# Duo attention and a two-layer MLP in one program: chunk order, V buffers, load order, and seven products in one more chunk

## The chip, the cores and the metric

The kernel runs on one core of a Trainium2 chip. A core has TensorE (PE) for matrix products, VectorE (DVE), ScalarE (ACT), GpSimd (POOL) and SyncE (SP), which work side by side and meet through semaphores. Transfers are issued by SP, ACT and POOL and are carried out by the core's 16 DMA engines. The metric is the device time of one execution in microseconds. Before the change its median is 223.92 us over three runs (223.15 to 224.44).

## The reference

Attention runs over 4 batches, 8 heads, 768 positions and 64 elements per head. Heads 0, 2 and 6 see all earlier positions; the other five see the first 4 positions (the sinks) and a window of 64. The attention's output, 3072 rows of 512, goes through two matrices with a leaky ReLU between them.

```python
scores = scale * np.matmul(q, k.transpose(0, 1, 3, 2))
causal = rel >= 0
stream_keep = causal & (is_sink | in_win)
mask = np.where(retr[0, :, 0, 0, None, None], full_mask, stream_mask)
a = np.exp(scores); a = a / (np.sum(a, axis=-1, keepdims=True) + 1e-09)
x = attn_out.transpose(0, 2, 1, 3).reshape(B * S, H * D)
h = x @ w_in                      # 512 -> 2048
g = np.maximum(0.01 * h, h)
return g @ w_out                  # 2048 -> 512
```

## The kernel before

**Chunks.** The rows are cut into 8 chunks of 384: two halves c = 0 and c = 1 of each batch. `ORDER` says which (batch, half) stands at which place. Before the change the order is, within each pair of batches, both first halves and then both second halves: (0,0) (1,0) (0,1) (1,1) (2,0) (3,0) (2,1) (3,1). A second half sees twice as many keys, so its attention is longer: a head that sees everything has five units (a unit is a product of queries and keys, an exponential, and later the product with V) where in a first half it has two. With the five window heads and one sink unit this makes 21 units in a second half and 12 in a first one.

**Stages of a chunk.** POOL loads Q, K and V and casts them (`load_qk`, `load_v`). SP turns K and Q with transposing transfers (`turn_dma`), VectorE spreads K into two zero-padded halves (`spreads`). SP copies V shifted by 64 rows into a second tile (`v_shift`, from `va` to `vb`), which the window heads need. Attention (`Attention.slots`) is a list of slots: slot t holds the score product and exponential of unit t, and the product with V of unit t - lag. When a pair of heads is done, VectorE divides by the row sums (`finish`, into `xs`), and SP turns the result into `xt` with a transposing transfer (`x_t`). Then comes the first matrix, `in_slots`: 16 ticks of four matmuls of 384 columns, each followed on ACT by the leaky ReLU into `g_all`. The second matrix runs in `Pair`s of two row tiles by a seven-product scheme (14 steps of four matmuls of 256 columns for a pair), with sums of `g_all` on VectorE, and its result goes out from the `o` tiles by SP.

**Seven products for the first matrix.** For the chunks in `BY_SEVEN` (6 and 7), half of the ticks, those of the first two groups of four column tiles, are replaced by a `Quad` each: seven units of four matmuls of 192 columns, with sums of w_in (`in_sums`, four on VectorE in pass 4, kept in the tiles of V buffer 1) and sums of xt (`x_sums`), copies on ACT and additions on VectorE.

**The order of work is written out by hand.** Each engine runs its instructions strictly in program order. Chunks 0 and 1 are written line by line. Then pass n, for n = 2 to 7 of the main loop (before.py, `for n in range(2, NCH)`), holds chunk n's first matrix (`ins`), the attention of chunk n+1 (`a`), the second matrix of what chunk n-1 completed (`outs`: one pair after an even chunk, two after an odd one), and the preparation of chunk n+2 and the loads of chunk n+3. `merge` spreads the slots of `a` evenly over the time of `ms`; the last microseconds of `ms` are kept back (`keep`) so that attention ends before the pass does. At the end of passes 3 and 4 POOL holds until the last `xt` of chunk n+1 has landed, and then issues Q and V of chunk n+3.

**Queues.** SP runs, for each pass, in order: the turning of K and Q of chunk n+2, the two shifted copies of its V, the four `xt` transposes of chunk n+1, the stores. An issue that waits holds what stands behind it. The same holds for POOL's loads. V has three buffers (batch 3 uses batch 0's).

**Lines** in the profile: L597 ticks, L679 units of a Quad, L771 and L792 steps of the second matrix, L357 and L392 score products, L326 products with V, L362 and L397 exponentials, L401 window masks, L425 `xs`, L430 `xt`, L248 turned K and Q, L153 and L154 shifted copies, L126 loads of V, L119 loads of K and Q, L143 loads of w_in, L637 and L646 sums of w_in and xt, L706 additions of a Quad, L600 the leaky ReLU, L826 stores.

Of the kernel before, what the change touches and what calls it, by code (L numbers as in the profile page):

```python
# [17 lines left out]
CH = 384  # L18
# [3 lines left out]
def kernel(  # L22
# [33 lines left out]

    ORDER = [(b + e, c) for b in range(0, B, 2) for c in range(2) for e in range(2)]

# [3 lines left out]
    def bf(name, *shape):  # L62
        return one.tile([128, *shape], BF16, name=name)
# [5 lines left out]
    ident = bf("ident", 128)  # L69
    blank = bf("blank", 256)  # L70
    diff = bf("diff", 128)
    half = one.tile([128, 2], FP32, name="half")
    m_caus = bf("m_caus", 128)
    n_caus = bf("n_caus", 128)
    n_one = bf("n_one", 64)
    n_first = bf("n_first", 128)
    m_one = bf("m_one", 64)
# [3 lines left out]
    hold = bf("hold", 1)  # L81
    shift = bf("shift", 2, 128)
    kt = [[bf(f"kt{i}_{hh}", 4, S) for hh in range(2)] for i in range(2)]
    va = [bf(f"va{i}", 6, H, D + 1) for i in range(3)]
    vb = [bf(f"vb{i}", 5, H - 1, D + 1) for i in range(3)]
    va.append(va[0])
    vb.append(vb[0])
    vs = [bf(f"vs{i}", H, D + 1) for i in range(2)]
# [13 lines left out]
    q0 = rot.tile([128, 3, H, D], BF16, name="q0", tag="qd", bufs=3)  # L102
    f0 = {nm: rot.tile([128, DM], FP32, name="o", tag="o", bufs=5).rearrange("p (h d) -> p h d", h=H) for nm in ("k", "q")}

# [136 lines left out]

    def turn_dma(n):
        qx[n] = rot.tile([128, 3, 4, 128], BF16, name="qd", tag="qd", bufs=3)
        raw["kx", n] = rot.tile([128, 3, 4, 128], BF16, name="kd", tag="kd", bufs=2)
        for nm, dst in (("k", raw["kx", n]), ("q", qx[n])):
            thirds = [slice(j, j + 1) for j in range(1 if nm == "q" and n == 3 else 3)]
            for g in thirds if n < 4 or (nm, n) == ("k", 4) else [slice(0, 3)]:
                nc.sync.dma_start_transpose(out=dst[:, g].rearrange("p g q t -> p (g q) t"),  # L248
                                            in_=raw[nm, n][:, g].rearrange("p g h d -> p (g h d)"))
# [333 lines left out]
    done = [0] * NCH  # L583
    BY_SEVEN = (6, 7)

# [7 lines left out]
    def in_slots(n, tags=("ph",)):  # L593
        def tick(t, tag=None):
            ph = bank(tag or tags[t % len(tags)], [128, 512], FP32)
            for g in range(KG):
                nc.tensor.matmul(ph[:, 0:CH], lhsT=w_in_bf[:, g, 128 * t : 128 * t + 128],  # L597
                                 rhs=xts[n][:, g, :] if n else xts[0][:, :, g, :], start=(g == 0), stop=(g == KG - 1))
            done[n] += 1
            nc.scalar.activation(out=g_all[:, slab(n) : slab(n) + 3, t, :],  # L600
                                 in_=ph[:, 0:CH].rearrange("p (j t) -> p j t", j=3), func=ACTF.Prelu, alpha=0.01)

        if n not in BY_SEVEN:
            return [costing(0.65, lambda t=t: tick(t)) for t in range(NG)]
        ticks = [costing(0.65, lambda t=t: tick(t)) for t in range(NG // 2, NG)]
        if n + 1 < NCH:
            ticks = [costing(0.65, lambda t=t: tick(t)) for t in range(NG // 2, NG)]
            r, left = [], []
            for k in range(2):
                *units, last = Quad(n, k, "ph").slots()  # L610
                for x, f in enumerate(units):
                    r += [f, *left] if x == 1 else [f]
                    if x in (0, 1, 2, 5):
                        r.append(ticks.pop(0))
                left = [last]
            return r + left

        both = zip(Quad(n, 0, "psS").slots(), Quad(n, 1, "po").slots())
        return [f for t, two in zip(ticks, both) for f in (t, *two)]

    KH = KG // 2
    in_sum = {}
    for i, t in ((1, va[1]), (3, vb[1])):
        t = t.rearrange("p g h d -> p (g h d)")[:, 0 : 2 * KH * 512].rearrange("p (x g c) -> p x g c", x=2, g=KH)
        in_sum[i], in_sum[i + 1] = t[:, 0], t[:, 1]

    def in_sums(i):


        def quarter(a, e):  # L630
            w = w_in_bf[:, KH * a : KH * a + KH, 0:1024].rearrange("p g (k e f) -> p g k e f", e=2, f=256)
            return w[:, :, :, e, :]

        part = lambda j: in_sum[j].rearrange("p g (k f) -> p g k f", f=256)
        x, y, op = {1: (quarter(0, 1), quarter(1, 1), ALU.add), 2: (part(1), quarter(0, 0), ALU.subtract),
                    3: (quarter(0, 0), quarter(0, 1), ALU.subtract), 4: (quarter(1, 0), part(2), ALU.subtract)}[i]
        nc.vector.tensor_tensor(part(i), x, y, op=op)  # L637
# [3 lines left out]
    def x_sums(n):  # L641
        x = xts[n].rearrange("p g (j e t) -> p g j e t", j=3, e=2)
        b = lambda a, e: x[:, KH * a : KH * a + KH, :, e, :]
        t = rot.tile([128, 4, KH, 3, 64], BF16, name="x_sum", tag="qb", bufs=1)
        for i, y, z in ((1, b(0, 1), b(0, 0)), (2, b(1, 1), t[:, 0]), (3, b(1, 1), b(0, 1)), (4, b(1, 0), t[:, 1])):
            nc.vector.tensor_tensor(t[:, i - 1], y, z, op=ALU.subtract)  # L646
        x_sum[n] = t
        temps[n] = [rot.tile([128, 2, CH], FP32, name=nm, tag=tag, bufs=bufs) for nm, tag, bufs in
                    (("p1s", "kd", 2), ("us", "kd", 2), ("u3s", "kb", 1))]

    class Quad:
# [9 lines left out]
        def unit(self, u):  # L661
# [6 lines left out]
            w = lambda a, e: w_in_bf[:, KH * a : KH * a + KH, 512 * k + 256 * e : 512 * k + 256 * e + 256]  # L668
            q = lambda i: in_sum[i][:, :, 256 * k : 256 * k + 256]
            lhs, rhs, at = {"P1": (w(0, 0), b(0, 0), "y"), "P2": (w(1, 0), b(1, 0), "a"), "P6": (q(2), t[:, 1], "y"),  # L670
# [21 lines left out]
        def empty(self, u, s):  # L692
            copy = lambda o: nc.scalar.activation(out=o, in_=s, func=ACTF.Copy)
            if u == "P1":
                self.left = 4
                self.p1, self.u, self.u3 = (t[:, self.k] for t in temps[self.n])
                copy(self.p1)
# [39 lines left out]
    class Pair:  # L737
# [42 lines left out]
        def unit_of_two(self, u, half, lo, hi):  # L780
# [17 lines left out]
            if u == "P1":  # L798
                self.o = [rot.tile([128, DM], FP32, name="o", tag="o", bufs=5) for _ in range(2)]
                self.p1 = self.temp("p1", 2)  # L800
# [27 lines left out]
        def empty(self, u, s, c0, c1):  # L828
            add = lambda o, t: nc.vector.tensor_tensor(o, s, t[:, c0:c1], op=ALU.add)
            if u == "P1":  # L830
                self.o = [rot.tile([128, DM], FP32, name="o", tag="o", bufs=5) for _ in range(2)]
                self.p1 = self.temp("p1", 2)
# [116 lines left out]
    load_qk(1, "q")  # L949
    load_in(768, 1024)  # L950
    load_v(1)
    load_in(1024, 1536)
    load_in(1536, 2048)
# [100 lines left out]
    p0 = in_slots(0)  # L1054
    a1 = Attention(1, score_tags=("py", "psS", "psS"), po_tags=("po", "po", "po", "py"), xt_eng="v").slots([0, 2, 6, 1, 3, 4, 5, 7], lag=6)

# [7 lines left out]
    for a in ats[2:]:  # L1064
        nc.vector.memset(a[:, :, 1:3, :], 0.0)
    run(a1[5:7])
    v_shift_pe(0, "ph", "v", 1)
    run(a1[7:8])
    v_shift_pe(1, "ph", "v", 1)
    run(a1[8:11], merge(p0[8:], a1[11:]))  # L1070
    nc.vector.tensor_copy(m_win[:], m_one.rearrange("p (o t) -> p o t", o=1).to_broadcast([128, 6, 64]))
    zero_keys(0, nc.vector, CH, S)
    zero_keys(1, nc.vector, CH, S)
    nc.vector.memset(va[2][:, :, :, D], 1.0)
    turn_dma(2)
# [11 lines left out]
    load_qk(4)  # L1087
    load_v(4)
    run(steps(1, ("P1",)))
# [18 lines left out]
    sp, keep = spreads(3), tail(m2[at:], a2[-7:])  # L1108
    run(keep[:-5], sp[:3], keep[-5:], sp[3:])

    for n in range(2, NCH):
        a, extra = [], ()
        if n + 2 < NCH:
            if ORDER[n + 2][1] == 0:
                load_sinks(ORDER[n + 2][0])
                sink_values(ORDER[n + 2][0], nc.gpsimd)
            turn_dma(n + 2)
            v_shift(n + 2)
            extra = spreads(n + 2)
            if n + 3 < NCH:  # L1120
                load_qk(n + 3, "k" if n > 2 else "kq")
                if n < 3:
                    load_v(n + 3)
        if n + 1 < NCH:
            a = Attention(n + 1, cross=True).slots(lag=2 if n > 3 else 3)
            a = into(a, extra) if n > 2 else a
        if n == 4:
            more = [lambda i=i: in_sums(i) for i in range(1, 5)]
            a = [f for j, s in enumerate(a) for f in ([s, more[j // 2 - 1]] if j in (2, 4, 6, 8) else [s])]
        ins = in_slots(n)  # L1130
# [4 lines left out]
        elif n == 4:  # L1135
            ms = outs[:8] + ins[:2] + merge(ins[2:], outs[8:-6]) + outs[-6:]
        elif n == 6:
# [6 lines left out]
        if n == 2:  # L1144
            run(ms[:1])
            ms = ms[1:]
            at = last_of(ms, 3.5)
            ms, keep = ms[:at], tail(ms[at:-2], a[-3:]) + ms[-2:]
            a = a[:-7] + [f for i in range(4) for f in (a[i - 7], *extra[2 * i : 2 * i + 2])]
        elif a:  # L1150
            at = last_of(ms, 3.2 if n == 3 else 5.8)
            ms, keep = ms[:at], ms[at:]
            if n > 4:
                keep.insert(1, a.pop())
        run(merge(ms, a), keep)
        if n in (3, 4):

            nc.gpsimd.tensor_copy(hold[0:1, :], xts[n + 1][0:1, 3, 0:1])
            if n > 2:
                load_qk(n + 3, "q")  # L1160
            load_v(n + 3)
# [37 lines left out]
```

## Time and profile before

| what | value |
|---|---|
| median of three runs | 223.92 us (223.15 to 224.44) |
| profiled execution, its own time | 225.39 us |
| its span, first to last instruction | 223.6 us |
| granted TensorE clock | 1.000 |
| TensorE busy | 214.8 us, 96% |
| ACT busy | 144.6 us, 65% |
| VectorE busy | 139.7 us, 62% |
| POOL busy | 72.3 us, 32% |
| read from HBM, written | 27.30 MB, 6.29 MB |
| chain that ended last, by engine | PE 66%, DMA 22%, POOL 8% |

The page lists busy times, the span in 40 slices, the DMA queues and a chain: from the last instruction back, at each step to what released it. Groups and timelines name a line, an engine, the tiles written and read, a count and a time; what stands after `<-` in brackets ended the idle time before the instruction. All times are microseconds from the span's start.

### The profile page before, as it was taken

How to read it: one execution, taken by the hardware profiler on the slowest of the kernel's cores; microseconds unless marked ns; L12 is line 12 of the kernel's file. 1: busy time of each engine (PE TensorE's matmuls, PEld its weight loads, DVE VectorE, ACT ScalarE, POOL GpSimd, SP SyncE). 2: the span in 40 equal slices, each digit the busy share in tenths (PEclk: the TensorE clock that was granted, in tenths of full speed). 3: DMA queues.
4: the chain of work that ended last, by engine and by line, in shares of the span. 5: the costliest groups of instructions: out<-in, count | busy, mean ns of one | idle time of the engine just before them, and what ended most of it. 6: DMA issues, size and time to landing. Idle time of an engine off the chain costs nothing.

```text
span 223.6 us, 5996 instructions
## 1 busy us (share of the span) xinstructions
PE 214.8 (96%) x2408; PEld 167.6 (75%) x2408; DVE 139.7 (62%) x383; ACT 144.6 (65%) x329; POOL 72.3 (32%) x89
## 2 busy tenths in 40 slices
PE   8899999999899899989999999999999999999994
PEld 5578766688698576876687777677787988888893
DVE  6686967949599355851775773455383756707653
ACT  4767947743686897367647644888658886487220
POOL 8988632079208512821419300800000000000000
PEclk9999999999999999999999999999999999999999
DMA  9999999999999999999999995999320130200222
GB/s 129 159 179 169 196 206 179 180 152 154 130 115 198 212 108 149 130 201 159 146 186 145 127 148 148 159 139 145 73 94 4 55 95 18 97 0 3 94 94 97
DMA packets 112203, 28.89 MB, mean 129 GB/s; under 512 B 102192, under 2 KB 109232, under 8 KB 112176
## 3 DMA queue, kind: packets, MB, share of 16 engines
q0 software_dynamic: 77552, 13.37, 88.7%
q1 hardware_dynamic: 33568, 14.88, 37.5%
q8 instruction: 19, 0.31, 0.6%
q10 hardware_dynamic: 1056, 0.26, 0.6%
q14 instruction: 8, 0.07, 0.1%
HBM read 27.30 MB, written 6.29 MB: 150 GB/s over the span
## 4 chain that ended last, share of the span: by engine, by line
PE 66%; DMA 22%; POOL 8%; issue 1%; ACT 1%; DVE 0%; POOLq 0%; ACTq 0%
PE ph L597 26%; PE py L792 18%; DMA va<-in_v_dram 6%; PE po L326 6%; DMA w_in_bf<-in_moe_w_in_dram 4%; POOL va L126 4%; PE psS L357 4%; DMA kb<-in_k_dram 3%; DMA kd<-kb 3%; DMA xt<-xs 3%; DMA vb<-va 2%; PE ph L679 2%; PE py L771 2%; PE po L792 2%; PE psS L392 1%
## 5 line engine op out<-in xcount | busy, mean ns | idle before, releaser
L597 PE MATMUL ph<-xt,w_in_bf 128*128 128x384 bf16 x384 | 75.7, 326 | 0.8 <-DMA xt<-xs 0.7
L600 ACT ACTIVATE g_all<-ph 128x384 bf16<-128x384 f32 x96 | 47.1, 490 | 27.3 <-PE ph L597 26.0
L597 PEld LDWEIGHTS <-w_in_bf 128*128 128x128 bf16 x416 | 37.4, 97 | 18.6 <-issue 0.7
L362 ACT ACTIVATE at<-psS 128x384 bf16<-128x384 f32 x76 | 35.8, 489 | 8.9 <-PE psS L357 5.4
L792 PEld LDWEIGHTS <-sum 128*128 128x128 bf16 x256 | 23.9, 98 | 4.4
L119 POOL DMA_DIRECT2D kb<-in_k_dram x21 | 18.8, 918 | 22.4 <-DMA kd<-kb 21.3
L357 PE MATMUL psS<-qd,kt 128*128 128x384 bf16 (+2 forms) x90 | 22.9, 294 | 0.0
L126 POOL DMA_DIRECT2D va<-in_v_dram x24 | 21.4, 914 | 1.4 <-DMA kb<-in_k_dram 1.4
L119 POOL DMA_DIRECT2D qb<-in_q_dram x21 | 18.6, 911 | 5.6 <-DMA w_in_bf<-in_moe_w_in_dram 2.5
L326 PE MATMUL po<-va,at 128*128 128x65 bf16 x228 | 19.5, 194 | 0.3 <-DMA va<-in_v_dram 0.3
L792 PEld LDWEIGHTS <-g_all 128*128 128x128 bf16 x192 | 17.8, 98 | 2.4
L326 PEld LDWEIGHTS <-at 128*128 128x128 bf16 x234 | 14.3, 98 | 4.3 <-DVE at L365 0.9
L264 DVE COPY kt<-kd 64x512 bf16<-64x512 bf16 x36 | 12.3, 350 | 8.4 <-DMA kd<-kb 8.1
L397 ACT ACTIVATE ats<-psS 128x384 bf16<-128x384 f32 x33 | 15.9, 490 | 2.5 <-PE psS L392 2.1
L401 DVE TENSOR_TENSOR ats<-ats,m_win 128x384 bf16<-128x384 bf16 x35 | 12.5, 360 | 7.9 <-ACT ats L397 7.3
L792 PE MATMUL py<-w_sum,sum 128*128 128x256 bf16 x120 | 17.4, 272 | 0.0
L753 DVE TENSOR_TENSOR sum<-g_all 128x1024 bf16<-128x1024 bf16 x24 | 16.4, 683 | 0.0
L792 PE MATMUL py<-w_out_bf,g_all 128*128 128x256 bf16 x112 | 16.1, 272 | 0.0
L792 PE MATMUL py<-w_out_bf,sum 128*128 128x256 bf16 x120 | 15.7, 272 | 0.0
L425 DVE TENSOR_TENSOR xs<-po,linv 128x384 bf16<-128x384 f32 x27 | 15.1, 558 | 0.9
L771 PEld LDWEIGHTS <-sum 128*128 128x128 bf16 x152 | 13.1, 98 | 1.6 <-issue 0.2
L326 PEld LDWEIGHTS <-ats 128*128 128x128 bf16 x210 | 10.1, 97 | 5.2 <-DVE ats L401 2.0
(248 smaller groups left out, 379.3 us busy)
## 6 DMA issues: line engine op xcount, KB each, us to landing
out_dram<-o SPq DMA_DIRECT2D x23, 256.0 KB, 3.3
va<-in_v_dram POOLq DMA_DIRECT2D x24, 128.0 KB, 8.0
kb<-in_k_dram POOLq DMA_DIRECT2D x21, 128.0 KB, 6.2
qb<-in_q_dram POOLq DMA_DIRECT2D x21, 128.0 KB, 7.4
w_out_bf<-in_moe_w_out_dram POOLq DMA_DIRECT2D x4, 512.0 KB, 13.0
w_in_bf<-in_moe_w_in_dram POOLq DMA_DIRECT2D x3, 512.0 KB, 8.4
vb<-va SPq DMA_DIRECT2D x8, 170.6 KB, 5.5
w_in_bf<-in_moe_w_in_dram POOLq DMA_DIRECT2D x2, 256.0 KB, 7.6
```

The lines of the kernel that those rows point to most:

```text
L119: nc.gpsimd.dma_start(out=t[:, g], in_=nat[nm][b, c, :, :, g])
L126: nc.gpsimd.dma_start(out=va[b][:, 3 * c + g, :, 0:D], in_=nat["v"][b, c, :, :, g])
L326: nc.tensor.matmul(o, lhsT=lhsT, rhs=rhs, start=first, stop=False, skip_group_check=True)
L357: nc.tensor.matmul(s[:, off : off + w], lhsT=kt[i][hh][:, p, 128 * kj : 128 * kj + 128], rhs=q_of(n, p, lo, CH), start=(j == 0), stop=(j = ...
L362: nc.scalar.activation(out=a[:, 0:off], in_=s[:, 0:off], func=ACTF.Exp, scale=SM)
L397: nc.scalar.activation(out=av_, in_=s[:, 0:CH].rearrange("p (j e f) -> p j e f", j=3, e=2), func=ACTF.Exp, scale=SM)
L425: nc.vector.tensor_tensor(xs[:], po[:, :, :, 0:D], linv.to_broadcast([128, 3, 2, D]), op=ALU.mult)
L597: nc.tensor.matmul(ph[:, 0:CH], lhsT=w_in_bf[:, g, 128 * t : 128 * t + 128], rhs=xts[n][:, g, :] if n else xts[0][:, :, g, :], start=(g == ...
L600: nc.scalar.activation(out=g_all[:, slab(n) : slab(n) + 3, t, :], in_=ph[:, 0:CH].rearrange("p (j t) -> p j t", j=3), func=ACTF.Prelu, alp ...
L753: nc.vector.tensor_tensor(self.s[i], x, y, op=op)
L771: nc.tensor.matmul(s[:, 0 : c1 - c0], lhsT=lhs[:, j, :], rhs=rhs[:, j, c0:c1], start=first and j == 0, stop=(j == NH - 1), skip_group_chec ...
L792: nc.tensor.matmul(s, lhsT=lhs[:, j, :], rhs=rhs[:, j, :], start=u in ("P1", "P2", "P5") and j == 0, stop=(j == NH - 1), skip_group_check= ...
```

## The change

- `ORDER` takes the last two batches one after the other: chunks 4 and 5 are the halves of batch 2, chunks 6 and 7 those of batch 3. Chunk 5 becomes a second half, chunk 6 a first one.
- V has two buffers. Batch 2 takes batch 0's, batch 3 batch 1's. V of chunk 4 is loaded after chunk 2's attention in the program; V of chunk 5 is loaded in pass 3, held on POOL until K of chunk 5 is turned.
- Shifted copies: those of chunk 4 are issued by ACT at the end of pass 2, those of chunk 5 by SP at the end of pass 3 behind chunk 4's `xt`, those of chunk 7 in pass 5 behind three of chunk 6's `xt`. K of chunk 7 is turned at the end of pass 4.
- Chunk 4 joins `BY_SEVEN`. The sums of w_in get tiles of their own and are made in pass 2, with chunk 3's attention; the sums of xt of chunk 4 are made in pass 4. Quads of chunks 4 and 6 take their scratch from three small tiles; the output of a unit stands one place earlier.
- The `o` tiles go from five to four; small constant tiles share the first scratch tile.
- Of w_in's third quarter the first half (columns 1024 to 1280) is loaded ahead of chunk 1's V; chunk 1's attention has lag 8 instead of 6, and its slots are interleaved with chunk 0's last ticks accordingly.
- Definitions for more than two Quads a chunk and for a second half of the w_in sums are there and are not used: every entry of `BY_SEVEN` is (0, 1).

```diff
-    ORDER = [(b + e, c) for b in range(0, B, 2) for c in range(2) for e in range(2)]
+    ORDER = [(0, 0), (1, 0), (0, 1), (1, 1), (2, 0), (2, 1), (3, 0), (3, 1)]
...
-    va = [bf(f"va{i}", 6, H, D + 1) for i in range(3)]
-    vb = [bf(f"vb{i}", 5, H - 1, D + 1) for i in range(3)]
-    va.append(va[0])
-    vb.append(vb[0])
+    va = [bf(f"va{i}", 6, H, D + 1) for i in range(2)] * 2
+    vb = [bf(f"vb{i}", 5, H - 1, D + 1) for i in range(2)] * 2
...
-    BY_SEVEN = (6, 7)
+    BY_SEVEN = {4: (0, 1), 6: (0, 1), 7: (0, 1)}
...
+        ks = BY_SEVEN.get(n, ())
+        ticks = [costing(0.65, lambda t=t: tick(t)) for t in range(NG) if t // 4 not in ks]
...
+        r, left = [], []
+        for k in ks:
+            *units, last = Quad(n, k, "ph").slots()
+            for x, f in enumerate(units):
+                r += [f, *left] if x == 0 else [f]
+                if x in (0, 1, 2, 5) and ticks:
+                    r.append(ticks.pop(0))
+            left = [last]
+        return r + left + ticks
...
-                self.o = [rot.tile([128, DM], FP32, name="o", tag="o", bufs=5) for _ in range(2)]
+                self.o = [rot.tile([128, DM], FP32, name="o", tag="o", bufs=4) for _ in range(2)]
...
     load_in(768, 1024)
+    load_in(1024, 1280)
     load_v(1)
-    load_in(1024, 1536)
+    load_in(1280, 1536)
...
-    a1 = Attention(1, ...).slots([0, 2, 6, 1, 3, 4, 5, 7], lag=6)
+    a1 = Attention(1, ...).slots([0, 2, 6, 1, 3, 4, 5, 7], lag=8)
...
-    run(a1[5:7])
+    run(a1[5:8], p0[8:9], a1[8:9])
     v_shift_pe(0, "ph", "v", 1)
-    run(a1[7:8])
+    run(a1[9:10])
     v_shift_pe(1, "ph", "v", 1)
-    run(a1[8:11], merge(p0[8:], a1[11:]))
+    run(a1[10:13], merge(p0[9:14], a1[13:-3]))
+    run(p0[14:15], a1[-3:-2], p0[15:], a1[-2:])
...
     load_qk(4)
-    load_v(4)
...
     run(keep[:-5], sp[:3], keep[-5:], sp[3:])
+    load_v(4)
...
-            turn_dma(n + 2)
-            v_shift(n + 2)
+            turn_dma(n + 2, "q" if n == 5 else "kq")
+            if n == 3:
+                load_v(n + 2, behind=raw["kx", n + 2][0:1, 0, 0, 0:1])
+            if n == 4:
+                v_shift(n + 2)
...
-                if n < 3:
-                    load_v(n + 3)
...
-        if n == 4:
-            more = [lambda i=i: in_sums(i) for i in range(1, 5)]
-            a = [f for j, s in enumerate(a) for f in ([s, more[j // 2 - 1]] if j in (2, 4, 6, 8) else [s])]
+        if n == 2:
+            a = [(lambda f=f, i=(6, 9, 12, 15).index(j): (f(), in_sums(0, i + 1))) if j in (6, 9, 12, 15) else f for j, f in enumerate(a)]
...
-            ms = outs[:8] + ins[:2] + merge(ins[2:], outs[8:-6]) + outs[-6:]
+            ms = outs[:7] + [costing(0.0, lambda: x_sums(4))] + outs[7:8] + ins[:2] + merge(ins[2:], outs[8:-6]) + outs[-6:]
...
+            keep.insert(2, lambda: v_shift(4, nc.scalar))
...
-        run(merge(ms, a), keep)
+        run(merge(ms, a))
+        if n in (3, 5):
+            v_shift(n + 2)
+        if n == 4:
+            turn_dma(7, "k")
+        run(keep)
```

More of the change, by code (lines that the diff above doesn't have):

```diff
@@ L69 @@
     ident = bf("ident", 128)
-    blank = bf("blank", 256)
+    first = rot.tile([128, 768], BF16, name="first", tag="p1q", bufs=1)
+    blank, n_caus, n_first = first[:, 0:256], first[:, 256:384], first[:, 384:512]
+    shift = first[:, 512:768].rearrange("p (e t) -> p e t", e=2)
     diff = bf("diff", 128)
@@ L73 @@
     m_caus = bf("m_caus", 128)
-    n_caus = bf("n_caus", 128)
     n_one = bf("n_one", 64)
-    n_first = bf("n_first", 128)
     m_one = bf("m_one", 64)
@@ L81 @@
     hold = bf("hold", 1)
-    shift = bf("shift", 2, 128)
     kt = [[bf(f"kt{i}_{hh}", 4, S) for hh in range(2)] for i in range(2)]
-    va = [bf(f"va{i}", 6, H, D + 1) for i in range(3)]
-    vb = [bf(f"vb{i}", 5, H - 1, D + 1) for i in range(3)]
-    va.append(va[0])
-    vb.append(vb[0])
+    va = [bf(f"va{i}", 6, H, D + 1) for i in range(2)] * 2
+    vb = [bf(f"vb{i}", 5, H - 1, D + 1) for i in range(2)] * 2
     vs = [bf(f"vs{i}", H, D + 1) for i in range(2)]
@@ L102 @@
     q0 = rot.tile([128, 3, H, D], BF16, name="q0", tag="qd", bufs=3)
-    f0 = {nm: rot.tile([128, DM], FP32, name="o", tag="o", bufs=5).rearrange("p (h d) -> p h d", h=H) for nm in ("k", "q")}
+    f0 = {nm: rot.tile([128, DM], FP32, name="o", tag="o", bufs=4).rearrange("p (h d) -> p h d", h=H) for nm in ("k", "q")}
     def load_first(nm):
@@ L240, in empty, with turn_dma @@
             move(eng, kt[0][h][:, :, 128 * j : 128 * j + 128], pt[:], h)
[L242 to L245, printed above, removed]
+    def turn_dma(n, nms="kq"):
+        for nm in nms:
+            dst = rot.tile([128, 3, 4, 128], BF16, name=f"{nm}d", tag=f"{nm}d", bufs=3 if nm == "q" else 2)
+            if nm == "q":
+                qx[n] = dst
+            else:
+                raw["kx", n] = dst
             thirds = [slice(j, j + 1) for j in range(1 if nm == "q" and n == 3 else 3)]
@@ L601, in tick @@
                                  in_=ph[:, 0:CH].rearrange("p (j t) -> p j t", j=3), func=ACTF.Prelu, alpha=0.01)
[L603 to L613, printed above, removed]
-                        r.append(ticks.pop(0))
-                left = [last]
-            return r + left
@@ L618, in in_slots @@
-        both = zip(Quad(n, 0, "psS").slots(), Quad(n, 1, "po").slots())
-        return [f for t, two in zip(ticks, both) for f in (t, *two)]
-    KH = KG // 2
[L622 to L627, printed above, removed]
+        ks = BY_SEVEN.get(n, ())
+        ticks = [costing(0.65, lambda t=t: tick(t)) for t in range(NG) if t // 4 not in ks]
@@ new lines, in in_slots @@
+        if n + 1 == NCH:
+            several = [Quad(n, k, tag).slots() for k, tag in zip(ks, ("psS", "po", "ph"))]
+            if len(ks) > 2:
+                r = []
+                for t in range(12):
+                    r += [fs[t - 2 * i] for i, fs in enumerate(several) if 0 <= t - 2 * i < 8]
+                    if t in (0, 1, 9, 10):
+                        r.append(ticks.pop(0))
+                return r
+            return [f for t, *fs in zip(ticks, *several) for f in (t, *fs)]
+        r, left = [], []
@@ new lines, in in_slots @@
+        for k in ks:
[6 more added lines that the diff above has]
+        return r + left + ticks
+    KH = KG // 2
+    in_sum, in_sum_of = {}, {}
+    for hf, (t1, t3) in enumerate(((one.tile([128, 2 * KH * 512], BF16, name="in_sum1"), one.tile([128, 2 * KH * 512], BF16, name="in_sum3")),
+                                     (va[0].rearrange("p g h d -> p (g h d)"), vb[0].rearrange("p g h d -> p (g h d)")))):
+        for i, t in ((1, t1), (3, t3)):
+            t = t[:, 0 : 2 * KH * 512].rearrange("p (x g c) -> p x g c", x=2, g=KH)
+            in_sum[hf, i], in_sum[hf, i + 1] = t[:, 0], t[:, 1]
@@ L630, in quarter, with in_sums @@
+    def in_sums(hf, i):
         def quarter(a, e):
-            w = w_in_bf[:, KH * a : KH * a + KH, 0:1024].rearrange("p g (k e f) -> p g k e f", e=2, f=256)
+            w = w_in_bf[:, KH * a : KH * a + KH, 1024 * hf : 1024 * hf + 1024].rearrange("p g (k e f) -> p g k e f", e=2, f=256)
             return w[:, :, :, e, :]
-        part = lambda j: in_sum[j].rearrange("p g (k f) -> p g k f", f=256)
+        part = lambda j: in_sum[hf, j].rearrange("p g (k f) -> p g k f", f=256)
         x, y, op = {1: (quarter(0, 1), quarter(1, 1), ALU.add), 2: (part(1), quarter(0, 0), ALU.subtract),
@@ L643, in x_sums @@
         b = lambda a, e: x[:, KH * a : KH * a + KH, :, e, :]
-        t = rot.tile([128, 4, KH, 3, 64], BF16, name="x_sum", tag="qb", bufs=1)
+        t = rot.tile([128, 4, KH, 3, 64], BF16, name="x_sum", tag="x_sum", bufs=1)
         for i, y, z in ((1, b(0, 1), b(0, 0)), (2, b(1, 1), t[:, 0]), (3, b(1, 1), b(0, 1)), (4, b(1, 0), t[:, 1])):
@@ L647, in x_sums @@
         x_sum[n] = t
-        temps[n] = [rot.tile([128, 2, CH], FP32, name=nm, tag=tag, bufs=bufs) for nm, tag, bufs in
-                    (("p1s", "kd", 2), ("us", "kd", 2), ("u3s", "kb", 1))]
+        if n + 1 == NCH:
+            temps[n] = [rot.tile([128, 2, CH], FP32, name=nm, tag=tag, bufs=bufs) for nm, tag, bufs in
+                        (("p1s", "kd", 2), ("us", "kd", 2), ("u3s", "kb", 1))]
     class Quad:
@@ L668, in unit @@
             w = lambda a, e: w_in_bf[:, KH * a : KH * a + KH, 512 * k + 256 * e : 512 * k + 256 * e + 256]
-            q = lambda i: in_sum[i][:, :, 256 * k : 256 * k + 256]
+            q = lambda i: in_sum[k // 2, i][:, :, 256 * (k % 2) : 256 * (k % 2) + 256]
             lhs, rhs, at = {"P1": (w(0, 0), b(0, 0), "y"), "P2": (w(1, 0), b(1, 0), "a"), "P6": (q(2), t[:, 1], "y"),
@@ L695, in empty @@
                 self.left = 4
-                self.p1, self.u, self.u3 = (t[:, self.k] for t in temps[self.n])
+                self.p1, self.u, self.u3 = (t[:, self.k] for t in temps[n]) if n in temps and self.k < 2 else \
+                    (rot.tile([128, CH], FP32, name=nm, tag=nm, bufs=1)[:] for nm in ("p1q", "uq", "u3q"))
                 copy(self.p1)
@@ L830, in empty @@
             if u == "P1":
-                self.o = [rot.tile([128, DM], FP32, name="o", tag="o", bufs=5) for _ in range(2)]
+                self.o = [rot.tile([128, DM], FP32, name="o", tag="o", bufs=4) for _ in range(2)]
                 self.p1 = self.temp("p1", 2)
@@ L1054 @@
     p0 = in_slots(0)
-    a1 = Attention(1, score_tags=("py", "psS", "psS"), po_tags=("po", "po", "po", "py"), xt_eng="v").slots([0, 2, 6, 1, 3, 4, 5, 7], lag=6)
+    a1 = Attention(1, score_tags=("py", "psS", "psS"), po_tags=("po", "po", "po", "py"), xt_eng="v").slots([0, 2, 6, 1, 3, 4, 5, 7], lag=8)
     run(a1[0:3])
@@ L1073 @@
     zero_keys(1, nc.vector, CH, S)
-    nc.vector.memset(va[2][:, :, :, D], 1.0)
     turn_dma(2)
@@ L1154 @@
                 keep.insert(1, a.pop())
-        run(merge(ms, a), keep)
+        run(merge(ms, a))
[4 more added lines that the diff above has]
+        run(keep)
         if n in (3, 4):
             nc.gpsimd.tensor_copy(hold[0:1, :], xts[n + 1][0:1, 3, 0:1])
-            if n > 2:
-                load_qk(n + 3, "q")
+            load_qk(n + 3, "q")
             load_v(n + 3)
```

## The prediction

> **What bounds the kernel now.** I read the page's totals first, then the chain that ended last, the waits of TensorE, and the timelines of TensorE and SyncE around each wait.
>
> ```profile
> PE 214.8 (96%) x2408; PEld 167.6 (75%) x2408; DVE 139.7 (62%) x383; ACT 144.6 (65%) x329; POOL 72.3 (32%) x89
> ...
> DMA  9999999999999999999999995999320130200222
> ```
>
> TensorE is busy 96% of the span. The DMA engines have work in every slice up to the 30th, about 168 us. So time can only come from TensorE's work or from the gaps in it. The chain shows two stretches.
>
> ```profile
> 38.93 7.39 DMA kd<-kb
> ...
> 56.48 13.87 DMA va<-in_v_dram
> 70.36 5.45 DMA vb<-va
> 75.94 0.34 PE po L326 x6
> ...
> 92.64 0.45 ACT at L362
> 93.08 6.46 DMA xt<-xs
> ```
>
> Up to 75.94 the chain runs through transfers: K of chunk 2, V of chunk 3 (landed 70.35), its shifted copy. TensorE then waits for that copy. After 75.94 the chain is TensorE, with one more transfer in it, the last transpose of chunk 3's attention output. TensorE's waits from 70 us to the end, and their places:
>
> ```profile
> PE po L326 <- DMA vb<-va: 0.7, 1, 0.7
> PE ph L597 <- DMA xt<-xs: 0.7, 1, 0.7
> ```
> ```profile
> 98.28 0.65 PE L597 MATMUL ph<-xt,w_in_bf 128*128 128x384 bf16 x3
> 99.59 0.32 PE L597 MATMUL ph<-xt,w_in_bf 128*128 128x384 bf16 x1 [0.66 <-DMA xt<-xs]
> ...
> 149.01 0.34 PE L392 MATMUL psS<-qd,kt 128*128 128x64 bf16 x6
> 149.41 0.20 PE L326 MATMUL po<-vb,ats 128*128 128x65 bf16 x1
> ```
>
> A four-matmul tick takes 0.65 us, 0.162 each, so the fourth matmul of the tick at 98.28 should start at 98.77; it starts at 99.59: 0.82 lost. In the same way the first loss, at 75.94, is 0.83. Around 146 to 149.4 three gaps of 0.18, 0.15 and 0.23 us come from exponentials and masks arriving late (six 64-column matmuls take 0.17 us, yet 149.01 to 149.41 is 0.40). These are what later edits can win back.
>
> **The change, part by part.**
>
> *Everything before 75.94* (one w_in quarter ahead of chunk 1's V, lag 8 in chunk 1's attention, the small tiles put together): nothing. The moved load is 256 KB; at the 196 to 206 GB/s of these slices, 1.3 us, so chunk 1's V lands 1.3 us later. Its first use moves later by two attention slots and a tick (0.65 us and more). The w_in half behind it lands no later. What hides either sign is the transfer chain above: its members keep their order on POOL and SP, and TensorE is 0.83 us early at 75.94. Bounds 0 to +0.5, taken 0.
>
> *Output tiles 5 to 4*: chunk pair 2's first write (ACT, o<-ph, 69.15) now waits for the store of pair 0, issued at 60.58 with 8.7 us to landing: 69.2. Behind it on ACT stands a copy at 70.19 with 0.66 idle before it. So 0 while the store isn't over 0.6 us later; bounds 0 to +0.5.
>
> *V of chunk 4* waits for chunk 2's attention, whose last V read is at 68.05; POOL issues these loads at 73.25 after Q of chunk 4, as before. Nothing. *Its shifted copy leaves SP for ACT.* SyncE's timeline before (start, length, line, what it issues):
>
> ```profile
> 80.66 5.17 SPq L248 DMA_TRANSPOSE qd<-qb  x1
> 85.94 0.64 SPq L153 DMA_DIRECT2D vb<-va  x1
> 87.44 0.59 SPq L154 DMA_DIRECT2D vb<-va  x1
> 88.14 6.19 SPq L430 DMA_TRANSPOSE xt<-xs  x4
> ```
>
> The second copy waited on SP for V until 87.44 and the four xt transposes stood behind it, about 1.25 us apart, the last at 93.08. The first three xs were ready by 83.3, the last at 89.98. Without the copies SP starts them at 85.9 and the last goes at 90.1. Chunk 5's V (93.81 to 96.47) no longer loads against it. With the 6.46 us of the old landing it is there at 96.6, before 98.77: the whole 0.82 goes (bounds 0 and -0.82). The Trainium skill ("DMA: Bandwidth & Descriptors", Issuing engines are not separate DMA queues) says that DMAs of all engines share the same 16 and another issuer saves issue time only. By it alone I would book nothing; the rows show an issuer held by a wait, so I book -0.82. On ACT the two issues (about 0.6 each) come after the g_all at 87.93, at 88.4, when V has landed (87.43); one g_all is behind them, then ACT idles 2.72 us: nothing. The copy, 3.5 us in this stretch, lands at about 93, and its reader comes at 95.64. Bounds 0 to +0.6.
>
> *The weight sums move to pass 2*: four of 0.69 = 2.7 us on VectorE, 14.6 busy of 23.65 from 75.94 to 99.59. Masks may come 0.69 later, but the products with V stand three slots behind. Bounds 0 to +0.5, taken 0.
>
> *Chunk 4 by seven products.* Two four-tile groups leave 8 ticks and become 14 units of four 192-column matmuls. From the chain, a unit of pass 6 and a tick, and from the answer on the units' line its weight loads (shortest, median, longest ns):
>
> ```profile
> 170.56 0.33 PE ph L679 x4
> ...
> 171.93 0.65 PE ph L597 x4
> ```
> ```profile
> L679 PEld LDWEIGHTS <-w_in_bf x48: 96/98/100, 165.1 to 201.0; 128*128 128x128 bf16 x48
> ```
>
> 28 x 82 ns = 2.30 against 16 x 162 = 2.59: -0.29 a group, -0.6 in all. Here a rule speaks against the change: "TensorE: Matmul & The Clock Gate" (LDWEIGHTS; Back-to-back issue gap) gives a 128-column weight load 107 ns (128 / 1.2) and lets both set the sustained spacing. At 107 a group would take 3.0 us, +0.4, so +0.8 in place of -0.6. The trace has loads of 98 ns under matmuls 82 ns apart in this very code: the row decides.
>
> *The order of chunks.* Pass 4 gets the attention with 21 exponential units instead of 12, pass 5 the 12. TensorE's sum is unchanged. Passes 4, 5 and 6 before (stretch, its length, then busy time and count of PE, PEld, DVE, ACT and POOL, the granted clock, which is full throughout, DMA share and GB/s):
>
> ```profile
> 111.44:140.74 29.30, 29.30 (x300) 22.92 (x299) 18.59 (x46) 16.80 (x40) 9.96 (x13) 1.00 1.59 149
> 140.74:164.30 23.56, 23.48 (x260) 17.05 (x259) 11.17 (x33) 17.46 (x42) 3.99 (x5) 1.00 1.24 119
> 164.30:193.00 28.70, 28.70 (x344) 24.21 (x342) 17.78 (x44) 21.58 (x51) 0.00 (x0) 1.00 0.18 55
> ```
>
> In pass 4 ACT gains 9 exponentials (4.4 us) and 14 copies and outputs for 8 g_all (+3.1): 24.3 in some 31 us, 78%. VectorE gains x sums 4 x 0.355, adds 6 x 0.555, loses 2.7: 20.6. Pass 6 before had this mix, ACT 75%, and lost nothing. Pass 5 had 74% and lost 0.56, because its 21 exponentials share so little TensorE work; it becomes light. I take -0.6 there and +0.2 in pass 4: -0.4 (bounds -0.6 and +0.6).
>
> *Chunk 5's V and shifted copy* come later: V waits on POOL for chunk 5's K transposed (before: landed 106.1; without V against it about 3 us sooner, 103). Then the hold copy (0.4) and three issues to 106, landing about 110.5. The copies stand on SP behind the four xt of chunk 4 (last issue then about 110), land at 115 to 117. Readers: pass 4 starts at 111.44 - 0.82 = 110.6; 8 output steps of 0.44, the first unit 0.33 and the attention slots between (3.6) put the first stream product at 118.1. Hidden by 1 to 3 us; this is the thin place. Behind the waiting copy on SP stand two stores, the sink rows and K and Q of chunk 6. Q and V of chunk 6 are held by chunk 4's xt as before. Chunk 7's copies now stand before chunk 6's last xt, but V of 7 (before: issued to 144.7, landed 154) comes no later: nothing.
>
> Sum: -0.82 - 0.6 - 0.4 = -1.8. The profiled execution took 225.39 with a span of 223.6 and 1.8 around it: span 221.8, execution 223.6. Its runs have the median 223.92, 1.5 lower, so 222.1.
>
> **Rivals.**
>
> *A, the sum holds: 222.1*, own range 221.3 to 222.8.
>
> *B, the gain turns into ACT and VectorE waits in pass 4.* For: units and ticks share the two banks of tag ph, and exponentials, g_all and copies queue on ACT, and pass 5 lost 0.56 at 74%. Against: pass 6 lost none. Tripling pass 5's loss costs 1.5: 223.6.
>
> *C, slower: chunk 5's V is late.*
>
> ```profile
> va<-in_v_dram POOLq DMA_DIRECT2D x24, 128.0 KB, 8.0
> ...
> vb<-va SPq DMA_DIRECT2D x8, 170.6 KB, 5.5
> ```
>
> If K of 5 still lands at 106.1, V is issued to 109.2, lands at 117.2 by the 8.0 median, and the copy at 117.2 + 0.6 + 5.5 = 123.3: 5.2 us after 118.1, 227.3. A stall begins when V lands after 112.0; it cancels the gain at 113.8, and from there the kernel is slower. Against: V alone waits then, where before it shared the stretch with K.
>
> *D, the change doesn't do what it says for xt* (last transpose still after 98.8): -1.0, 222.9. *E, more is won*: the 0.83 at 75.94 goes too, 221.2.
>
> **How the numbers follow.** A 0.57, B 0.15, C 0.18, D 0.06, E 0.04. Half a per cent is 1.1 us, about what runs of this kernel can tell (223.15 to 224.44). Faster, under 222.8: A nearly whole, E, some of D: 0.61. Same, to 225.0: B, the rest, the mild end of C: 0.21. Slower: 0.18. The range leaves out the ends of C and E: 221.0 to 225.5.
>
> **What would show it.** Right: no TensorE wait for xt in pass 3; the last xt of chunk 3 issued near 90; 56 matmuls of 192 columns in chunk 4, 82 ns apart; the 0.83 at 75.94 still there; no gaps in pass 5. Wrong: a TensorE wait for vb near 117 (C), ACT without gaps in pass 4 and TensorE waiting for it (B), or a wait for a store or for V before 70 that outlasts the 0.83.

## The result

The changed kernel takes 223.02 us (median of 21 runs, 221.28 to 224.71) against 224.56 us (21 runs, 223.15 to 227.76): ratio 0.993, 95% interval 0.9902 to 0.9959, so 1.5 us or 0.7% faster. The prediction was 222.1 from 223.92, a gain of 1.8. The absolute figure came out 0.9 higher than that, of which 0.6 is the kernel before itself: 224.56 in 21 runs where three had given 223.92. The profiled execution took 221.28 us with a span of 219.4; that of before took 225.39 with 223.6. These two lie 4.1 us apart, more than twice what the medians do, and most of this section and the next is about that difference. The ratios leave out executions over 1.5% above the fastest of their kernel (14 of the 35 of before in the series of the next section), so they are not the quotients of the medians given beside them.

From the page of the changed kernel: the totals, the row of DMA slices, and the shares of the chain.

```profile
PE 212.3 (97%) x2432; PEld 168.7 (77%) x2432; DVE 144.5 (66%) x392; ACT 147.0 (67%) x335; POOL 72.6 (33%) x91
...
DMA  9999999999999999999999996993320131200222
...
PE 88%; DMA 6%; POOL 2%; DVE 1%; issue 1%; POOLq 0%
```

TensorE is still the engine that is always busy, 97% of a shorter span where it was 96%. The chain is now 88% TensorE; its 6% of DMA is V of chunk 0 and lies before 28 us. The list of TensorE's waits in the changed kernel, complete (engine, line, tile, releaser, us in total, times, longest):

```profile
PE psS L156 <- DVE first L939: 1.1, 1, 1.1
PE py L230 <- ACT q L992: 0.9, 1, 0.9
PE psS L528 <- DVE qf L203: 0.8, 2, 0.4
PE po L326 <- DMA va<-in_v_dram: 0.3, 1, 0.3
PE ph L722 <- ACT g_all L726: 0.2, 1, 0.2
PE py L172 <- DMA va<-in_v_dram: 0.2, 1, 0.2
```

All of them lie in the first 30 us. The two entries shown of before, the shifted copy (vb) at 75.94 and xt at 99.59, are gone. SyncE's queue around pass 2, to be held against the rows of before in the prediction:

```profile
78.28 4.11 SPq L248 DMA_TRANSPOSE qd<-qb  x1
82.50 6.84 SPq L430 DMA_TRANSPOSE xt<-xs  x4
89.44 1.26 SPq L834 DMA_DIRECT2D out_dram<-o  x2
```

No vb stands between Q and xt. The last xt was issued at 88.01 and landed at 94.56; the matmul that reads it first, the fourth of the tick at 96.01, starts at 96.50 without a wait: four matmuls of 0.162 each and no bracket.

```profile
96.01 0.81 PE L597 MATMUL ph<-xt,w_in_bf 128*128 128x384 bf16 x4
```

The stretches of passes 2, 4 and 5 in the changed kernel (columns as before: stretch, its length, busy us and count of PE, PEld, DVE, ACT and POOL, granted clock, DMA share, GB/s):

```profile
73.92:96.90 22.98, 22.98 (x285) 17.65 (x284) 16.55 (x44) 16.88 (x40) 8.25 (x10) 1.00 1.84 168
108.41:139.65 31.24, 31.24 (x365) 26.33 (x364) 21.43 (x54) 22.83 (x55) 12.89 (x17) 1.00 1.56 153
139.65:159.93 20.28, 20.28 (x219) 14.97 (x218) 10.69 (x33) 13.92 (x33) 1.66 (x2) 1.00 0.90 115
```

In all three TensorE's busy time equals the stretch; before, pass 5 had 23.48 of 23.56. Pass 4 took in the larger attention and the seven products: ACT 22.83 of 31.24 (73%; estimated 24.3), VectorE 21.43 (estimated 20.6), no wait.

**Where 4.2 us of span went.** At 59.4 us the two first profiles are still together. TensorE around the first product of chunk 2 with the shifted copy of V, before:

```profile
59.40 0.34 PE L392 MATMUL psS<-qd,kt 128*128 128x64 bf16 x6
60.75 0.19 PE L326 MATMUL po<-vb,ats 128*128 128x65 bf16 x1 [1.01 <-DVE ats L401]
```

and changed:

```profile
59.31 0.34 PE L392 MATMUL psS<-qd,kt 128*128 128x64 bf16 x6
59.52 0.19 PE L326 MATMUL po<-vb,ats 128*128 128x65 bf16 x1
```

Six 64-column matmuls take 0.17 us, so before lost 1.18 here and the changed kernel nothing. The profile names VectorE's mask, but that was done by 59.05 in the one (58.69 + 0.36) and 58.96 in the other; what the product also reads is the shifted copy, issued by SyncE at 52.97 and at 53.02. The mask before:

```profile
58.69 0.36 DVE L401 TENSOR_TENSOR ats<-ats,m_win 128x384 bf16<-128x384 bf16 x1 [1.27 <-ACT ats L397]
```

So the same copy, issued at the same time, came by 59.5 in one execution and not before about 60.7 in the other. This wait was missed in the prediction. TensorE's losses after 55 us, each the start of a matmul less the start of the one before it and that one's usual spacing, in the two first profiles and the four of the experiments (those that stand alike in all six are left out, and so are other gaps of less than 0.1 us, which come to 0.3 to 0.4 more in the two profiles of before; the row of chunk 4's matmuls is a count, 32 of 162 ns less 56 of 82):

| us | before | before, again | changed | changed, again | without chunk 4's seven | copy of chunk 4 on SyncE |
|---|---|---|---|---|---|---|
| shifted copy of chunk 2, about 60 | 1.18 | 1.76 | 0 | 0.07 | 0.07 | 2.14 |
| shifted copy of chunk 3, about 76 | 0.83 | 0 | 0 | 0 | 0 | 0 |
| a product of chunk 2, 63.5 | 0 | 0 | 0.17 | 0.17 | 0.17 | 0 |
| mask of chunk 3, about 78 | 0 | 0 | 0 | 0.18 | 0.18 | 0 |
| mask of chunk 3, about 88 | 0.14 | 0 | 0 | 0 | 0.50 | 0 |
| last xt of chunk 3, about 99 | 0.83 | 1.55 | 0 | 0 | 0 | 0.83 |
| mask of chunk 4, about 108 | 0 | 0.37 | 0 | 0 | 0 | 0 |
| shifted copy of chunk 5, about 116 | 0 | 0 | 0 | 0.13 | 0 | 0 |
| three gaps of pass 5 | 0.56 | 0.56 | 0 | 0 | 0 | 0 |
| chunk 4's matmuls, over the changed kernel | 0.6 | 0.6 | 0 | 0 | 0.6 | 0 |
| TensorE's lag at the first vb product, over the changed kernel | 0.09 | 1.01 | 0 | 0.01 | 0.81 | 0.28 |
| sum, over that of the changed kernel | 4.1 | 5.7 | 0 | 0.4 | 2.2 | 3.1 |
| span less 219.4 | 4.2 | 5.7 | 0 | 0.4 | 2.2 | 3.1 |

The sums close to 0.1 us; the small gaps left out are about made up for by the time after the last matmul's start, 0.2 to 0.4 longer in the four profiles of the changed kernel and its variants. Three rows are the prediction's sum: xt 0.83, matmuls 0.6, pass 5 0.56, together 2.0 where 1.8 was put. The other 2.0 between the first two profiles are the first two rows.

### The profile page after: what moved, and what is told of

Its sections match the earlier page's. It is cut to its first block, busy times and chain, and to the rows that moved or that the text cites. A ratio compares the mean times of both kernels' runs of the same rounds, so it can differ in the third digit from the quotient of the medians.

```text
span 219.4 us, 6062 instructions
## 1 busy us (share of the span) xinstructions
PE 212.3 (97%) x2432; PEld 168.7 (77%) x2432; DVE 144.5 (66%) x392; ACT 147.0 (67%) x335; POOL 72.6 (33%) x91
## 4 chain that ended last, share of the span: by engine, by line
PE 88%; DMA 6%; POOL 2%; DVE 1%; issue 1%; POOLq 0%
PE ph L597 26%; PE py L800 20%; PE po L326 8%; PE py L779 8%; DMA va<-in_v_dram 6%; PE psS L357 5%; PE ph L686 4%; PE psS L392 3%; PE psS L597 2%; PE po L779 2%; PE po L800 2%; PE ph L779 1%; POOL va L123 1%; PE psS L686 1%; PE po L686 1%; PE psS L779 1%
## 5 line engine op out<-in xcount | busy, mean ns | idle before, releaser
L597 PE MATMUL ph<-xt,w_in_bf 128*128 128x384 bf16 x352 | 68.9, 326 | 0.0
L600 ACT ACTIVATE g_all<-ph 128x384 bf16<-128x384 f32 x88 | 43.4, 493 | 21.1 <-PE ph L597 18.5
L597 PEld LDWEIGHTS <-w_in_bf 128*128 128x128 bf16 x384 | 34.0, 97 | 17.4 <-issue 0.9
L123 POOL DMA_DIRECT2D va<-in_v_dram x24 | 21.4, 914 | 0.9 <-DVE xs L573 0.7
L401 DVE TENSOR_TENSOR ats<-ats,m_win 128x384 bf16<-128x384 bf16 x35 | 13.1, 375 | 10.0 <-ACT ats L397 9.8
```

What stands on the lines that cost most here:

```text
L123: nc.gpsimd.dma_start(out=va[b][:, 3 * c + g, :, 0:D], in_=nat["v"][b, c, :, :, g])
```

## The experiments

Theory: the gain is the xt wait (0.8), the seven products (0.6) and pass 5's gaps (0.4 to 0.6); the first two rows of the table vary from execution to execution with the transfers and are no work of the edits. Rival: the edits before 76 us (the moved quarter of w_in, the lag, the interleaving) brought about half of it. The four kernels were timed in one series in which before had the median 226.0 (35 runs).

**Before, again.** No edit.

> The kernel before, once more. In its first profile TensorE lost 1.18 us at 60.75 and 0.83 us at 75.94, behind V of chunk 3 that landed at 70.35; in the profile of the changed kernel V of chunk 3, issued at the same microsecond, landed at 67.03 and both losses were gone. Theory (landings of these transfers vary from execution to execution, the edits have no part in it): this profile has V of chunk 3 landed anywhere from 66 to 71, and the two losses sum to anything from 0 to 2; ratio 1.00. Rival (the early edits made the transfers land earlier): V of chunk 3 lands at 69.5 or later again and the losses sum to 1.5 or more.

225.01 us, ratio 1.0003 (0.9956 to 1.0049); span 225.1. V of chunk 3 landed at 68.99. Two of TensorE's waits and three steps of the chain in this execution:

```profile
PE po L326 <- DMA vb<-va: 1.6, 1, 1.6
PE ph L597 <- DMA xt<-xs: 1.4, 1, 1.4
```
```profile
40.90 7.38 DMA kd<-kb
...
50.42 4.73 DMA va<-in_v_dram
55.17 6.95 DMA vb<-va
```

The wait near 60 is back and now named as what it is: K of chunk 2 transposed, V of chunk 2 behind it, its shifted copy behind that. The one at 75.94 is not there, since TensorE had already lost 1.76. So these two waits come from one chain of transfers, and what TensorE loses at the first shortens the second. V of chunk 3 landed a little earlier than the rival had it (69.5), and the losses of 1.76 fit both: this run alone does not decide. It shows that the xt wait (1.55) and the three gaps of pass 5 (0.18, 0.15, 0.23, the same as in the first profile) belong to the kernel.

**Changed, again.** No edit.

> The changed kernel, once more. Theory of varying landings: V of chunk 3 lands from 66 to 71 and the two losses are back in part; ratio 0.993 as before. Rival (the early edits): V of chunk 3 lands before 67.5 and no loss at either place. By both: no wait of TensorE for the transposed attention of chunk 3, 56 matmuls of 192 columns in chunk 4, no gaps in pass 5.

222.73 us, ratio 0.989 (0.985 to 0.9929); span 219.8. V of chunk 3 landed at 67.82, a little later than the rival had it (67.5), and the two losses were 0.07 together, as the rival said. One new loss, TensorE in pass 4:

```profile
115.95 0.33 PE L357 MATMUL psS<-qd,kt 128*128 128x384 bf16 x1
116.25 0.19 PE L326 MATMUL po<-vb,ats 128*128 128x65 bf16 x1
```

A 384-column matmul takes 0.162, so the product could have started at 116.12. Its mask was done at 115.37; SyncE had issued the shifted copies of chunk 5 behind the four xt of chunk 4:

```profile
101.22 6.84 SPq L430 DMA_TRANSPOSE xt<-xs  x4
108.31 0.65 SPq L150 DMA_DIRECT2D vb<-va  x1
109.46 0.59 SPq L151 DMA_DIRECT2D vb<-va  x1
```

The first of them landed at 115.28; the second, issued 1.15 later, is what remains for the product at 116.25 to have waited for. This is rival C's place, with 0.13 us.

**Chunk 4 without the seven products.**

```
-    BY_SEVEN = {4: (0, 1), 6: (0, 1), 7: (0, 1)}
+    BY_SEVEN = {6: (0, 1), 7: (0, 1)}
-            ms = outs[:7] + [costing(0.0, lambda: x_sums(4))] + outs[7:8] + ins[:2] + ...
+            ms = outs[:8] + ins[:2] + ...
```

> The changed kernel with chunk 4 by plain ticks (no seven products, no x sums for it); all else as changed. By the trace's spacing of 82 ns: 0.6 us slower than the changed kernel, 223.6 against 223.0. By the weight load of 107 ns as the spacing: 0.8 us faster, 222.2. If the copies and adds of the seven products make TensorE wait in pass 4 (rival B): faster than 223.0 too, with gaps of the changed kernel in pass 4 gone.

223.71 us, ratio 0.9938 (0.9893 to 0.9984): 1.0 us slower than the changed kernel of the same series by the medians, 1.1 by the ratios. The intervals overlap, so the time gives the sign only as likely; it does speak against the 0.8 faster that was estimated from the 107 ns of the weight-load rule that the prediction cites. The spacing itself is read in the changed kernel, a unit of chunk 4 and what follows it:

```profile
115.48 0.49 PE L686 MATMUL ph<-xt,w_in_bf 128*128 128x192 bf16 x4
115.81 0.33 PE L357 MATMUL psS<-qd,kt 128*128 128x384 bf16 x1
```

Four in 0.33 us, 82 ns each; the weight loads of these units in pass 4 have 95 to 98 ns and lie under the matmuls. 56 of them in place of 32 of 162 ns are 5.18 - 4.59 = 0.6. TensorE's waits for ACT or VectorE in pass 4 are none with the seven products and none without: rival B has nothing to stand on. The execution profiled here shows one loss that the others don't, at 88.16; VectorE and TensorE before it:

```profile
87.12 0.59 DVE L264 COPY kt<-kd 64x512 bf16<-64x512 bf16 x2 [0.76 <-DMA kd<-kb]
87.74 0.36 DVE L401 TENSOR_TENSOR ats<-ats,m_win 128x384 bf16<-128x384 bf16 x1
```
```profile
88.16 0.20 PE L326 MATMUL po<-vb,ats 128*128 128x65 bf16 x1 [0.34 <-DVE ats L401]
```

K of chunk 4 transposed landed late (87.09; 83.66 in the changed kernel), its spreading copies stood on VectorE ahead of a mask, and the product waited for the mask. The 0.37 at 108 in the repeat of before is the same with K of chunk 5.

**The copy of chunk 4 back on SyncE.**

```
             if n == 4:
-            if n == 4:
+            if n in (2, 4):
                 v_shift(n + 2)
-            keep.insert(2, lambda: v_shift(4, nc.scalar))
```

> The changed kernel with the shifted copy of chunk 4 issued by SyncE at the head of pass 2, ahead of the four xt transposes, as before; all else as changed. If SyncE's wait for V was what made xt late: V of chunk 4 now lands at 83.8, when SyncE is free, so the copies hold it only for their two issues (1.3 us); the last xt lands at 95.5 to 96.6 and its reader comes at about 96.8: 0 to 0.4 us slower than the changed kernel. If the issues themselves or the copies' traffic in the shared DMA engines made xt late: 0.8 us slower, 223.8, with the wait for xt back at 0.8.

223.42 us, ratio 0.9956 (0.9913 to 0.9999): 0.7 us slower than the changed kernel by the medians, 1.5 by the ratios, again with overlapping intervals, so the time alone decides nothing. Two of TensorE's waits, SyncE's queue, and the chain through the early part:

```profile
PE po L326 <- DMA vb<-va: 2.0, 1, 2.0
...
PE ph L597 <- DMA xt<-xs: 0.7, 1, 0.7
```
```profile
82.53 2.80 SPq L248 DMA_TRANSPOSE qd<-qb  x1
86.04 0.63 SPq L150 DMA_DIRECT2D vb<-va  x1
87.34 0.59 SPq L151 DMA_DIRECT2D vb<-va  x1
88.04 5.88 SPq L430 DMA_TRANSPOSE xt<-xs  x4
```
```profile
39.31 8.38 DMA kd<-kb
...
49.96 4.56 DMA va<-in_v_dram
54.54 7.22 DMA vb<-va
```

The xt wait is back at 0.83. My expectation of 0 to 0.4 took V of chunk 4 to land at 83.8; here it landed at 87.33. Its load was issued 1.7 us later than in the changed kernel (74.92 against 73.19), behind the early loss, and took 1.8 longer to land. To be set beside it is the kernel without chunk 4's seven products, where V landed at 87.15, nearly the same, and the copies were on ACT:

```profile
82.05 2.90 SPq L248 DMA_TRANSPOSE qd<-qb  x1
85.06 6.31 SPq L430 DMA_TRANSPOSE xt<-xs  x4
```

There xt starts 3.0 us earlier, the last lands at 96.06 (99.37 here), and TensorE does not wait. The same copies and the same late V; up to there the programs differ in the issuer alone. The last transpose took about as long from issue to landing in both (6.70 here, 6.04 there), so it was not the traffic that made it late: SyncE's queue held it, and rival D is settled. Of the 2.7 us between Q (issued to 85.33) and the first xt (88.04), 1.2 are the two issues and 1.5 are waits: each copy started within 0.05 of the landing of its part of V, at 85.99 and 87.33. Without the waits the last xt would have landed at about 97.9, an estimate from these figures, and its reader was due at 98.58. So the waits did it, and copies on SyncE should cost nothing when V comes early; that was not measured.

The second thing that this run shows is in its early part. Up to SyncE's copies at 86 us its instructions on every engine are those of the changed kernel, in the same order, the early edits with them. It lost 2.14 where the others with the same instructions lost 0, 0.07 and 0.07. K of chunk 2 took 8.4 us from its first issue to the release of V (7.5 in the changed kernel), and the shifted copy 7.2 (at most 6.5). So the loss near 60 comes and goes with the execution: that part of the theory is shown. Whether the early edits make it rarer (none or nearly none in 3 of 4 executions with them, 1.8 and 2.0 in both without) six executions can't say. Over all timed runs before spreads from 222.83 to 228.76 us (68 runs) and the changed kernel from 221.28 to 225.65 (33 runs), which would fit losses that come more often in before; these runs have no profiles to show it.

Not tried: the early edits alone or undone, the old order of chunks on two V buffers, and the copy on ACT as the only edit to the kernel before.

## Why the prediction was right, point by point

- **xt, -0.82: right.** The last transpose of chunk 3 was to be issued at 90.1; it was at 88.01 in an execution 2.1 us ahead by then. The wait is absent in all three profiles with the copy on ACT and there in all three (0.83, 1.55, 0.83) with it on SyncE. The rule weighed there, that another issuer saves issue time only, did not decide: with the copies on SyncE 1.5 of 2.7 us on its queue were waits. The copy landed at 93.07, as said.
- **Seven products, -0.6: right,** 82 ns a matmul and 32 x 162 less 56 x 82 ns in the count. The +0.8 estimated from the rule did not come: loads of 95 to 98 ns under matmuls 82 ns apart again.
- **Order, -0.4: right in sign, it was 0.56.** The three gaps of pass 5 stand alike in both profiles of before and in none of four with the new order; the cost in pass 4 (+0.2) did not come. That the order is the cause is argued from this, no run isolated it.
- **Pass 4's engines:** ACT 22.8 for 24.3, VectorE 21.4 for 20.6, 31.2 us for "some 31". Rival B was weighed fairly and did not come.
- **Everything before 75.94, 0: not refuted, but for a wrong reason.** I read one binding point, the 0.83 at 75.94, and said that it would still be there. It was not, neither in the four profiles with the edits nor in the repeat of before. Rival E had it gone, with a chance of 0.04 and 221.2 us (221.3 by its own sum); the first profiled execution, 221.28, is there, the median of 223.02 is not. The step that failed is the reading of the wait at 60.75: I took the released-by name (a mask) and did not see the shifted copy of chunk 2, 1.18 late. This chain goes from K of chunk 2 to two successive waits, worth 0 to 2.1 us by the execution. The times leave no room for a systematic gain of 2 us there: 1.5 in the first series and, by the ratio of 0.989, 2.5 in the second, where the three other terms make 2.0 to 2.7 (xt 0.83 to 1.55). Over all runs, though, the medians of the second series lie 3.3 apart, and 12 more runs of before in it had 225.01 where the other 35 had 226.0. So up to about a microsecond is left open, and that the first series came within 0.3 of the 1.8 is in part luck.
- **Output tiles 5 to 4, 0: right.** The first write of pair 2 waited for the store as said (ACT, 1.49 idle until 68.69; 69.2 was put), with no wait of TensorE behind it.
- **Weight sums in pass 2, 0: right.** They ran at 73.7 to 80.6 and cost nothing in the changed kernel's profile; the 0.18 at 78 in two others, behind the second of them, is within the bound of 0.5 and is told of below. Larger were the losses by masks behind K's spreading copies, which I had not named.
- **Chunk 5's copy, hidden by 1 to 3 us: right in sign, mis-sized.** V landed at 107.0, 109.4, 110.6 and 111.3 in four executions (110.5 was put), always inside the 112.0 of rival C. But in the first profile the reader came at 116.0 and not at 118.1, because pass 4 began at 108.41 and not at 110.6, the early losses being gone, and the copies took 4.5 to 7.0 us from issue to landing where 5.5 was put. The margin can be nothing: in one execution of four the reader waited 0.13.

## What to carry to other kernels

An in-order issuing queue is a resource of its own: ask which instruction on it waits, and move the waiting one to an engine that is free at that time, even if all transfers share the same hardware. A releaser named at a wait is a guess; look at when it ended, and at every other operand of the waiting instruction, above all at copies. Before a difference between two profiles is explained by an edit, profile each program again: here 2 us of the 4.2 between the first pair came and went with the same instructions.

## What the runs showed of the hardware that was not expected

The same chain of transfers (K of chunk 2 transposed, V, shifted copy; same instructions, same order) took from 39.0 to at most 59.5 us in one execution and from 39.3 to 61.8 in another: 2 us more in 21, at granted clocks of 1.00 and 0.998. TensorE's gaps behind ACT and VectorE in pass 5 do not vary so: they came out as 0.18, 0.15 and 0.23 us in both executions of before.

VectorE and GpSimd held each other up. GpSimd and VectorE about 76 us in the repeat of the changed kernel:

```profile
76.28 1.33 POOL L133 TENSOR_TENSOR vs<-vsf,m_sink 128x448 bf16<-128x448 f32 x1 [0.45 <-DVE xs L425]
```
```profile
76.13 0.68 DVE L643 TENSOR_TENSOR in_sum<-in_sum,w_in_bf 128x1024 bf16<-128x1024 bf16 x1
76.73 0.96 DVE L367 TENSOR_TENSOR at<-at,m_caus 128x128 bf16<-128x128 bf16 x1
```

A mask of this shape takes 0.23 elsewhere; here it took 0.96 and ended at 77.69, just after GpSimd's sink values (77.61), which themselves took 1.33 (1.03 in the first profile) and had started under the weight sum. In the first profile GpSimd began first, ran until 76.85, and there the weight sum took 1.28 in place of 0.68 and the mask 0.21:

```profile
75.82 1.03 POOL L133 TENSOR_TENSOR vs<-vsf,m_sink 128x448 bf16<-128x448 f32 x1
```
```profile
76.12 1.28 DVE L643 TENSOR_TENSOR in_sum<-in_sum,w_in_bf 128x1024 bf16<-128x1024 bf16 x1
```

The product behind the mask of 0.96 is the one that lost 0.18 at 78 in the repeat; GpSimd's own spans are rough in these profiles. The Trainium skill ("SBUF — State Buffer", SBUF: two separate sides) says that a VectorE operation with two inputs in SBUF and a GpSimd operation that reads SBUF share a pair of ports which the first holds for its whole instruction while the other is blocked; these rows agree. The weight sums' bound in the prediction (0 to +0.5) did not come from there, and should have.
